# Loading the first 512 tokens of an attention and feed-forward kernel in longer rows

## The chip, the cores and the metric

The kernel runs on one core of a Trainium2 chip. The metric is device time in microseconds (us) of one launch. A core has five engines that run side by side and wait for each other through semaphores: PE (TensorE, matrix products and transposes; its weight loads are a row of their own, PEld), DVE (VectorE), ACT (ScalarE), POOL (GpSimd) and SP (SyncE, which here only issues transfers). Transfers between HBM and the on-chip memory run on 16 DMA engines.

## What is computed

Attention inside chunks of 64 tokens, for 8 batches of 8 heads, 576 tokens and 64 features, and then a feed-forward layer with a squared ReLU over all 4608 tokens:

```python
B, H, S, D = q.shape            # 8, 8, 576, 64; float32
q_c = q.reshape(B, H, S // 64, 64, D)          # k, v likewise
scores = (1 / sqrt(D)) * matmul(q_c, k_c.transpose(0, 1, 2, 4, 3))
attn = softmax(scores, axis=-1)
a = matmul(attn, v_c).reshape(B, H, S, D)
x = a.transpose(0, 2, 1, 3).reshape(B * S, H * D)   # 4608 x 512
out = maximum(x @ w_in, 0) ** 2 @ w_out             # d_ff 2048; float32 out
```

## The kernel before

The tokens are numbered through all batches and cut into 18 groups of 256 (`GT`). Two groups make a block of 512 tokens; there are nine: groups 0 and 1, then 3 and 2, then 4 and 5, and so on. For each block the kernel does the attention of its groups, and then the two products of the feed-forward layer: `ffn_in` (L316 on PE, ReLU on ACT at L322, square on DVE at L323, 16 steps) and `ffn_out` (L332), for block 0 `ffn_out_by_ft` (L361). The output leaves through ACT copies and POOL's DMAs.

The attention of a group has these steps. q and k come in as float32 in `q_sb` and `k_sb`, the values in `v_even` (even heads) and `v_odd` (odd heads, shifted by 64 tokens so that the chunks of both kinds lie on different halves of the partitions); each row of values carries an element 1.0 behind its 64 features, so that the product gives the sum of the softmax as well. q and k are turned so that the features lie on partitions (`qkT`). For groups 0 to 3 PE does this on the upper halves of the float32 words, read as bfloat16 (L164), and DVE and ACT copy it out of PSUM (L173). For later groups POOL casts (L212) and a transposing DMA does the rest (L219). `scores` makes 32 products of 64x64 (L233) and one exponential on ACT (L240). `values` makes, for each of the two tiles of 128 tokens, 16 products of 64x65 (L257), a reciprocal (L264) and a product (L265) on DVE, which gives `x`. `x` is transposed into `xT`, by PE for groups 0 to 5 (L195 and L284), by a transposing DMA from group 6 on (L278).

The order of everything is written out by hand: each engine works through its instructions in program order. At the beginning the loads of groups 0 and 1 are issued on SP's queue (q, k of group 0, of group 1, then the values of both), then the first piece of `w_in`, and then PE goes through the attention of groups 0 and 1. Between the steps stand fillers, `keep_busy(n)`: n products of the identity with itself, 128 columns each, whose result nobody reads. Then come the rest of `w_in` (8 pieces in all, cast to bfloat16 by POOL at L139) and `w_out` (8 pieces, L147) through five staging buffers (`w_st`), and the loads of group 3 and 2. After that the blocks follow, with the attention of the next block and the loads of the one after it spliced into slots of the feed-forward steps.

For groups 0 to 3 two neighbouring tokens of a head lie on one partition (512 B in HBM, one row of a transfer); the copy out of PSUM puts the tokens back in order. For later groups a row of q or k is one token of a head, 256 B, as are the rows of the values in all groups. The number of rows of a transfer is partitions x heads. All loads are issued by SP, in program order.

The text below names these: `qk_pieces` (L102, L110) and `v_pieces` (L117, L124) issue the loads, `load_w_in` (L136, L139) and `load_w_out` (L144, L147) the weights, `transpose_qk` is called as TE for groups 0 and 1, TA for group 3 and TM for group 2.

Of the kernel before, what the change touches and what calls it, by code (L numbers as in the profile page):

```python
# [10 lines left out]
FP32 = mybir.dt.float32  # L11
BF16 = mybir.dt.bfloat16
AF = mybir.ActivationFunctionType
ALU = mybir.AluOpType
# [3 lines left out]
def kernel(  # L18
# [9 lines left out]
    nc = tc.nc  # L28

    B, H, S, D = q.shape  # L30
    n_tokens = B * S
# [3 lines left out]
    n_hp = H // 2  # L35
    n_dt = d_model // 128
    n_ft = d_ff // 128
    GT = 256
    n_grp = n_tokens // GT

    blocks = [[0, 1], [3, 2]] + [[g, g + 1] for g in range(4, n_grp, 2)]
    FIRST_DMA_T = 4
    FIRST_DMA_X = 6
    BT = GT * max(len(b) for b in blocks)

    const_pool = ctx.enter_context(tc.tile_pool(name="const", bufs=1))
# [7 lines left out]

    ctx.enter_context(tc.manual_schedule())

    ident_f32 = const_pool.tile([128, 128], FP32, name="ident_f32")
    make_identity(nc, ident_f32)
    ident = const_pool.tile([128, 128], BF16, name="ident")
# [7 lines left out]
    NO = 2 * NV + 1  # L67
    v_even = [w_pool.tile([128, 2, n_hp, D + 1], FP32, name=f"ve_sb{i}") for i in range(NV)]
    v_odd = [w_pool.tile([128, n_hp, D + 1], FP32, name=f"vo_sb{i}") for i in range(NO)]
    for vt in v_even:  # L70
        nc.gpsimd.memset(vt[:, :, :, D:D + 1], 1.0)
    for vt in v_odd:
# [2 lines left out]
    def segments(g0, n):  # L75
        while n:
            b, s = divmod(g0, S)
            m = min(n, S - s)
            yield b, s, m
            g0 += m  # L80
            n -= m
# [9 lines left out]
                p += m  # L91

    def qk_pieces(g):
        q_sb = in_pool.tile([128, 2, H, D], FP32, name="q_sb")
        k_sb = in_pool.tile([128, 2, H, D], FP32, name="k_sb")
        qk[g] = (q_sb, k_sb)
        if g < FIRST_DMA_T:

            p = 0
            for b, s, m in segments(g * GT, GT):  # L100
                for dst, src in ((q_sb, q), (k_sb, k)):
                    yield lambda dst=dst, src=src, b=b, s=s, p=p, m=m: nc.sync.dma_start(  # L102
                        out=dst.rearrange("p t h d -> p (t h d)")[p:p + m // 2, :].rearrange(
                            "p (h e) -> p h e", h=H),
                        in_=src[b, :, s:s + m, :].rearrange("h (s i) d -> s h (i d)", i=2))
                p += m // 2
            return
        for t, p, m, b, s in runs(g):
            for dst, src in ((q_sb, q), (k_sb, k)):
                yield lambda dst=dst, src=src, b=b, s=s, t=t, p=p, m=m: nc.sync.dma_start(  # L110
                    out=dst[p:p + m, t, :, :],
                    in_=src[b, :, s:s + m, :].rearrange("h s d -> s h d"))

    def v_pieces(g):

        for t, p, m, b, s in runs(g):
            yield lambda t=t, p=p, m=m, b=b, s=s: nc.sync.dma_start(  # L117
                out=v_even[g % NV][p:p + m, t, :, 0:D],
                in_=v[b, 0::2, s:s + m, :].rearrange("h s d -> s h d"))
        for n in {0: [0, 1, 2], 2: [5], 3: [6, 7, 8]}.get(g, [2 * g + 1, 2 * g + 2]):  # L120
            lo, hi = max(0, 128 * n - 64), min(n_tokens, 128 * n + 64)
            p = lo - (128 * n - 64)
            for b, s, m in segments(lo, hi - lo):
                yield lambda n=n, p=p, m=m, b=b, s=s: nc.sync.dma_start(  # L124
                    out=v_odd[n % NO][p:p + m, :, 0:D],
                    in_=v[b, 1::2, s:s + m, :].rearrange("h s d -> s h d"))
                p += m
# [47 lines left out]
    def transpose_qk(g, q_pool, k_pool):  # L175
        qkT = att_pool.tile([128, 2, 2, n_hp, 128], BF16, name="qkT", bufs=4)
        state["qkT", g] = qkT
        for which, pool in enumerate((q_pool, k_pool)):
            copy = nc.scalar.copy if which else nc.vector.tensor_copy
            if pool is ps_ffn:  # L180
                bank = pool.tile([128, 512], FP32, name="ps_ffn")
            else:
                bank = pool.tile([128, 1024], FP32, name="ps_att")
            bank = bank.bitcast(BF16)[:, 0:1024]
            transpose_paired(g, which, bank)
            copy_paired(copy, qkT[:, which], bank)

    def transpose_x_early(g, t):
        j, c = place[g]
        if j not in xTs:  # L190
            xTs[j] = att_pool.tile([128, BT // 128, n_dt, 128], BF16, name="xT", bufs=2)
        psb = ps_ffn.tile([128, 512], FP32, name="ps_ffn").bitcast(BF16)
        x = state["x", g]
        for hp in range(n_hp):
            nc.tensor.transpose(  # L195
                out=psb[:, hp * 128:(hp + 1) * 128],
                in_=x[:, t, hp].rearrange("p a d -> p (a d)"),
                identity=ident)
        copy = nc.vector.tensor_copy if t else nc.scalar.copy
        copy(  # L200
            out=xTs[j][:, c // 128 + t].rearrange("p h q -> p (h q)"), in_=psb[:, 0:512])

    def keep_busy(n):
        ps = ps_ffn.tile([128, 512], FP32, name="ps_ffn")
        for _ in range(n):
            nc.tensor.matmul(out=ps[:, 0:128], lhsT=ident, rhs=ident, start=True, stop=True)

    def cast_qk(g):
        qkb = att_pool.tile([128, 2, 2 * H * D], BF16, name="qkb", bufs=2)
# [13 lines left out]
    def scores(g):  # L223
        qkT = state.pop(("qkT", g))
        ps = ps_att.tile([128, 1024], FP32, name="ps_att")
        for hp in range(n_hp):
            for t in range(2):
                for a in range(2):
                    for p in range(2):
                        c = p ^ a  # L230
                        cols = slice(p * 64, p * 64 + 64)
                        o0 = a * 512 + hp * 128 + t * 64
                        nc.tensor.matmul(  # L233
                            out=ps[64 * c:64 * c + 64, o0:o0 + 64],
                            lhsT=qkT[64 * a:64 * a + 64, 1, t, hp, cols],
                            rhs=qkT[64 * a:64 * a + 64, 0, t, hp, cols],
                            start=True, stop=True)
        e = att_pool.tile([128, 2, n_hp, 2, 64], BF16, name="e")
        state["e", g] = e
        nc.scalar.activation(  # L240
            out=e.rearrange("p a h t q -> p (a h t q)"), in_=ps, func=AF.Exp, scale=scale)

    def values(g, tiles=(0, 1)):
        e = state["e", g]
        veb = v_even[g % NV].bitcast(BF16)
        vob = [v_odd[(2 * g + n) % NO].bitcast(BF16) for n in range(3)]
        if 0 in tiles:
            state["x", g] = att_pool.tile([128, 2, n_hp, 2, D], BF16, name="x", bufs=3)
        x = state["x", g]
        for t in tiles:  # L250
            ps = ps_att.tile([128, 2, 512], FP32, name="ps_att")
            for hp in range(n_hp):
                for a in range(2):
                    for p in range(2):
                        c = p ^ a
                        vb = vob[t + p] if a else veb[:, t]
                        nc.tensor.matmul(  # L257
                            out=ps[64 * p:64 * p + 64, a, hp * (D + 1):(hp + 1) * (D + 1)],
                            lhsT=e[64 * c:64 * c + 64, a, hp, t, :],
                            rhs=vb[64 * c:64 * c + 64, hp, 1::2],  # L260
                            start=True, stop=True)
            o = ps[:, :, 0:n_hp * (D + 1)].rearrange("p a (h d) -> p a h d", d=D + 1)
            rec = att_pool.tile([128, 2, n_hp], FP32, name="rec", bufs=4)
            nc.vector.reciprocal(out=rec, in_=o[:, :, :, D])  # L264
            nc.vector.tensor_tensor(  # L265
                out=x[:, t].rearrange("p h a d -> p a h d"),
                in0=o[:, :, :, 0:D],
                in1=rec.to_broadcast([128, 2, n_hp, D]),
                op=ALU.mult)
# [24 lines left out]
    def TA(g):  # L294
        transpose_qk(g, ps_att, ps_att)

    def TE(g):
        transpose_qk(g, ps_ffn, ps_ffn)

    def TM(g):  # L300
        transpose_qk(g, ps_att, ps_ffn)

    def XE(g):
        for t in range(2):
            transpose_x_early(g, t)

    gTs = {}

# [76 lines left out]

    go(pieces([0, 1]))
    load_w_in(0, n_cast=2)
    TE(0)
    keep_busy(8)
    SC(0)  # L390
    keep_busy(6)
    TE(1)
    keep_busy(8)
    SC(1)
    keep_busy(10)
    AV(0, [0])
    keep_busy(4)
    AV(0, [1])
    keep_busy(8)
    transpose_x_early(0, 0)  # L400
    keep_busy(10)
    transpose_x_early(0, 1)
    AV(1, [0])
    keep_busy(8)
    AV(1, [1])
    transpose_x_early(1, 0)
    keep_busy(14)
    transpose_x_early(1, 1)
    keep_busy(10)

    for i in range(1, 8):
        load_w_in(i)
# [90 lines left out]
```

The softmax here doesn't subtract the row's maximum and nothing guards it: scores larger than these inputs give would overflow.

## Time and profile before

| | |
|---|---|
| median of 8 runs | 297.78 us |
| lowest and highest | 295.26 and 303.7 us |
| profiled execution, device time | 303.7 us |
| its span, first to last instruction | 301.9 us |
| its mean granted PE clock | 0.986 |
| PE, DVE, ACT, POOL busy | 284.8, 113.9, 131.0, 67.7 us |
| HBM read, written | 36.70, 9.44 MB |
| first L164 on PE | 4.99 us |
| first cast of `w_in` on POOL | 18.25 us |
| first L316 of block 0 | 20.13 us |

The profile is of one execution, the slowest of the eight; times in it count from its first instruction. The busy share of an engine says how much of the span it worked, not whether it was waited for; that is told by the waits and by the chain that ended last. In the rows by slice the span is cut into 40 equal parts of 7.5 us and a digit is a busy share in tenths. In the view by windows each engine has its busy time in the stretch and, in brackets, its instructions; then come the granted PE clock, the mean busy share of the DMA engines and the rate in GB/s.

### The profile page before, as it was taken

The page shows a single profiled execution, that of the slowest core. Times are in us where ns is not written, and L with a number is a line of the kernel's source. Part 1 is how long each engine was busy: PE and PEld are TensorE (multiplying, and loading weights), DVE is VectorE, ACT ScalarE, POOL GpSimd, SP SyncE. Part 2 cuts the span into 40 slices and gives each one's busy share as a digit, 9 for nine tenths or more (in the row PEclk, how much of TensorE's full clock was granted, in tenths as well). Part 3 has the DMA queues.
Part 4 walks back from the last instruction along what each step waited for, and adds up shares of the span by engine and source line. Part 5 has one row for each costly group of instructions (what it writes and reads, how often), then busy time and mean ns, then how long its engine had stood idle before and what let it go on. Part 6 is the DMA issues. An engine that isn't in the chain of part 4 may idle for free.

```text
span 301.9 us, 6460 instructions
## 1 busy us (share of the span) xinstructions
PE 284.8 (94%) x2630; PEld 142.4 (47%) x2630; DVE 113.9 (38%) x246; ACT 131.0 (43%) x226; POOL 67.7 (22%) x103
## 2 busy tenths in 40 slices
PE   2899998999899995999999999999999999999994
PEld 2674454885444442344444444444444444444441
DVE  1258514682434520247026604540563045205300
ACT  1536414773337511373157315721671267126511
POOL 2047724140070061032206013201320100010010
PEclk9999999999999999699999999999999999999998
DMA  7999999999999999999999699779996600310011
GB/s 208 217 322 363 362 292 244 241 215 204 207 213 208 226 228 209 230 201 182 208 262 223 124 257 253 151 149 267 226 164 134 181 35 14 92 72 35 0 69 69
DMA packets 156141, 57.03 MB, mean 189 GB/s; under 512 B 139281, under 2 KB 151825, under 8 KB 156113
## 3 DMA queue, kind: packets, MB, share of 16 engines
q1 hardware_dynamic: 153168, 47.33, 75.1%
q0 software_dynamic: 2800, 9.18, 9.1%
q8 instruction: 20, 0.33, 0.5%
q10 hardware_dynamic: 144, 0.13, 0.1%
q14 instruction: 9, 0.07, 0.1%
HBM read 36.70 MB, written 9.44 MB: 153 GB/s over the span
## 4 chain that ended last, share of the span: by engine, by line
PE 75%; DMA 12%; SPq 8%; DVE 1%; issue 1%; POOL 1%; ACT 0%; ACTq 0%
PE ps_ffn L316 37%; PE ps_ffn L332 34%; DMA w_st<-in_moe_w_in_dram 4%; DMA k_sb<-in_k_dram 2%; SPq L124 2%; DMA w_st<-in_moe_w_out_dram 2%; SPq L102 2%; DMA xT<-x 2%; PE ps_att L257 2%; SPq L117 2%; PE ps_att L233 2%; DMA qkT<-qkb 1%; SPq L136 1%; POOL w_in_bf L139 1%; DVE gT L323 1%
## 5 line engine op out<-in xcount | busy, mean ns | idle before, releaser
L316 PE MATMUL ps_ffn<-xT,w_in_bf 128*128 128x512 bf16 (+1 forms) x640 | 131.8, 363 | 4.0 <-DMA xT<-x 3.3
L323 DVE TENSOR_TENSOR gT<-rl 128x512 bf16<-128x512 bf16 (+1 forms) x160 | 76.5, 492 | 132.9 <-ACT rl L322 130.7
L332 PE MATMUL ps_ffn<-w_out_bf,gT 128*128 128x512 bf16 x512 | 112.9, 379 | 0.0
L322 ACT ACTIVATE rl<-ps_ffn 128x512 bf16<-128x512 f32 (+1 forms) x160 | 86.6, 557 | 44.2 <-PE ps_ffn L316 38.7
L316 PEld LDWEIGHTS <-w_in_bf 128*128 128x128 bf16 x640 | 61.8, 99 | 65.9 <-issue 4.8
L332 PEld LDWEIGHTS <-gT 128*128 128x128 bf16 x512 | 49.3, 98 | 58.0
L349 ACT COPY o_sb<-ps_ffn 128x512 f32<-128x512 f32 x31 | 18.2, 586 | 91.5 <-PE ps_ffn L332 91.5
L350 POOL DMA_DIRECT2D out_dram<-o_sb x31 | 16.7, 539 | 141.8 <-ACT o_sb L349 141.8
L212 POOL CAST qkb<-q_sb 128x1024 bf16<-128x1024 f32 x14 | 14.8, 1057 | 52.9 <-DMA q_sb<-in_q_dram 48.2
L265 DVE TENSOR_TENSOR x<-ps_att,rec 128x512 bf16<-128x512 f32 x36 | 24.9, 692 | 1.2
L240 ACT ACTIVATE e<-ps_att 128x1024 bf16<-128x1024 f32 x18 | 17.9, 1023 | 5.3 <-PE ps_att L233 5.2
L212 POOL CAST qkb<-k_sb 128x1024 bf16<-128x1024 f32 x14 | 15.5, 1110 | 2.5 <-DMA k_sb<-in_k_dram 2.3
L361 PE MATMUL ps_ffn<-w_out_bf,gT 128*128 128x512 bf16 x64 | 14.7, 379 | 0.0
L264 DVE RECIPROCAL rec<-ps_att 128x8 f32<-128x8 f32 x36 | 7.2, 200 | 16.6 <-PE ps_att L257 16.6
L139 POOL CAST w_in_bf<-w_st 128x1024 bf16<-128x1024 f32 (+1 forms) x9 | 8.6, 959 | 19.4 <-DMA w_st<-in_moe_w_in_dram 19.4
L257 PEld LDWEIGHTS <-e 64*64 64x64 bf16 x576 | 6.6, 107 | 8.3 <-issue 2.3
L147 POOL CAST w_out_bf<-w_st 128x1024 bf16<-128x1024 f32 x8 | 8.9, 1112 | 7.2 <-DMA w_st<-in_moe_w_out_dram 7.1
L257 PE MATMUL ps_att<-vo_sb,e 64*64 64x65 bf16 x288 | 9.1, 196 | 1.0 <-DMA vo_sb<-in_v_dram 1.0
L361 PEld LDWEIGHTS <-gT 128*128 128x128 bf16 x64 | 6.0, 98 | 7.2 <-DVE gT L323 0.3
L257 PE MATMUL ps_att<-ve_sb,e 64*64 64x65 bf16 x288 | 9.1, 197 | 0.0
L233 PE MATMUL ps_att<-qkT 64*64 64x64 bf16 x576 | 7.7, 197 | 1.4 <-DMA qkT<-qkb 1.0
L233 PEld LDWEIGHTS <-qkT 64*64 64x64 bf16 x576 | 6.0, 110 | 6.2 <-issue 3.2
(34 smaller groups left out, 53.4 us busy)
## 6 DMA issues: line engine op xcount, KB each, us to landing
out_dram<-o_sb POOLq DMA_DIRECT2D x35, 256.0 KB, 4.1
q_sb<-in_q_dram SPq DMA_DIRECT2D x25, 256.0 KB, 5.0
k_sb<-in_k_dram SPq DMA_DIRECT2D x25, 256.0 KB, 5.0
ve_sb<-in_v_dram SPq DMA_DIRECT2D x32, 128.0 KB, 4.1
vo_sb<-in_v_dram SPq DMA_DIRECT2D x32, 128.0 KB, 3.7
w_st<-in_moe_w_in_dram SPq DMA_DIRECT2D x8, 512.0 KB, 6.5
w_st<-in_moe_w_out_dram SPq DMA_DIRECT2D x8, 512.0 KB, 6.6
q_sb<-in_q_dram SPq DMA_DIRECT2D x3, 512.0 KB, 6.7
```

The lines of the kernel that those rows point to most:

```text
L212: nc.gpsimd.tensor_copy(out=qkb[:, which], in_=qk[g][which].rearrange("p t h d -> p (t h d)"))
L233: nc.tensor.matmul(out=ps[64 * c:64 * c + 64, o0:o0 + 64], lhsT=qkT[64 * a:64 * a + 64, 1, t, hp, cols], rhs=qkT[64 * a:64 * a + 64, 0, t, ...
L240: nc.scalar.activation(out=e.rearrange("p a h t q -> p (a h t q)"), in_=ps, func=AF.Exp, scale=scale)
L257: nc.tensor.matmul(out=ps[64 * p:64 * p + 64, a, hp * (D + 1):(hp + 1) * (D + 1)], lhsT=e[64 * c:64 * c + 64, a, hp, t, :], rhs=vb[64 * c: ...
L265: nc.vector.tensor_tensor(out=x[:, t].rearrange("p h a d -> p a h d"), in0=o[:, :, :, 0:D], in1=rec.to_broadcast([128, 2, n_hp, D]), op=AL ...
L316: nc.tensor.matmul(out=h[:, 0:n], lhsT=w_in_bf[:, dt, ft * 128:(ft + 1) * 128], rhs=xT[:, c // 128:(c + n) // 128, dt, :], start=(dt == 0) ...
L322: nc.scalar.activation(out=rl[:, 0:n], in_=h[:, 0:n], func=AF.Relu)
L323: nc.vector.tensor_tensor(out=gT[:, ft, c:c + n], in0=rl[:, 0:n], in1=rl[:, 0:n], op=ALU.mult)
L332: nc.tensor.matmul(out=o_ps, lhsT=gT[:, ft, tt * 128:(tt + 1) * 128], rhs=w_out_bf[:, ft, :], start=(ft == 0), stop=(ft == n_ft - 1))
L349: nc.scalar.copy(out=o_sb, in_=o_ps)
L350: nc.gpsimd.dma_start(out=out[t0:t0 + 128, :], in_=o_sb)
L361: nc.tensor.matmul(out=o_ps[tt], lhsT=gT[:, ft, tt * 128:(tt + 1) * 128], rhs=w_out_bf[:, ft, :], start=(ft == 0), stop=(ft == n_ft - 1))
```

## The change

Only the first 512 tokens (groups 0 and 1) are treated differently.

- q of both groups comes in one transfer of 128 partitions, four neighbouring tokens of a head on one partition (1 KB rows), and so does k. `qk[0]` is q of 512 tokens, `qk[1]` is k. Both lie in `qk_sb`, which for the other groups holds q and k of one group as two halves.
- The values of a group come in one transfer, two neighbouring tokens of a head on one partition (512 B rows), all heads together, in `v_pair`. A row has an element 1.0 at its front and at its end.
- `transpose_both` does what TE did, for q of both groups and then for k of both: 32 transposes into two PSUM banks, copied by DVE (bank 0) and ACT (bank 1), once per group.
- Since a partition of `v_pair` holds an even and an odd token, the keys of a chunk of 64 are split into 32 even and 32 odd ones. `scores` makes 64 products of 64x32 (32 keys) for 64 queries each instead of 32. `values` makes for a tile 32 products over 32 keys, which accumulate, and four products of zeros ahead of them that clear the accumulators; the two columns of ones give two partial sums, which a reduction on DVE adds ahead of the reciprocal.
- `keep_busy` multiplies zeros, 512 columns wide, and its counts are others: 12 of them stand ahead of the first transpose.
- The part of `v_odd` that group 1 loaded for group 2 (64 tokens) is loaded with group 2's values.
- SP issues 4 transfers ahead of the first piece of `w_in` instead of 13.

```diff
@@ tiles
+    zeros = const_pool.tile([128, 512], BF16, name="zeros")
+    nc.gpsimd.memset(zeros, 0.0)
+    v_pair = [w_pool.tile([128, H, 2 * D + 2], FP32, name=f"vp_sb{i}")
+              for i in range(N_PAIRED)]
+    for vt in v_pair:
+        nc.gpsimd.memset(vt[:, :, 0:1], 1.0)
+        nc.gpsimd.memset(vt[:, :, 2 * D + 1:2 * D + 2], 1.0)
@@ qk_pieces
-        q_sb = in_pool.tile([128, 2, H, D], FP32, name="q_sb")
-        k_sb = in_pool.tile([128, 2, H, D], FP32, name="k_sb")
+        qk_sb = in_pool.tile([128, 2, 2, H, D], FP32, name="qk_sb")
+        if g < 2:
+            qk[g] = qk_sb.rearrange("p w t h d -> p (w t h d)").rearrange(
+                "p (h e) -> p h e", h=H)
+            p = 0
+            for b, s, m in segments(0, 2 * GT):
+                yield lambda dst=qk[g], src=(q, k)[g], b=b, s=s, p=p, m=m: nc.sync.dma_start(
+                    out=dst[p:p + m // 4],
+                    in_=src[b, :, s:s + m, :].rearrange("h (s i) d -> s h (i d)", i=4))
+                p += m // 4
+            return
+        q_sb, k_sb = qk_sb[:, 0], qk_sb[:, 1]
@@ v_pieces
+        if g < N_PAIRED:
+            p = 0
+            for b, s, m in segments(g * GT, GT):
+                yield lambda b=b, s=s, p=p, m=m: nc.sync.dma_start(
+                    out=v_pair[g][p:p + m // 2, :, 1:2 * D + 1],
+                    in_=v[b, :, s:s + m, :].rearrange("h (s i) d -> s h (i d)", i=2))
+                p += m // 2
+            return
-        for n in {0: [0, 1, 2], 2: [5], 3: [6, 7, 8]}.get(g, [2 * g + 1, 2 * g + 2]):
-            lo, hi = max(0, 128 * n - 64), min(n_tokens, 128 * n + 64)
+        for n in {2: [4, 5], 3: [6, 7, 8]}.get(g, [2 * g + 1, 2 * g + 2]):
+            lo, hi = max(N_PAIRED * GT, 128 * n - 64), min(n_tokens, 128 * n + 64)
@@ new: q (which = 0) or k (which = 1) of groups 0 and 1
+    def transpose_both(which):
+        nh = n_hp // 2
+        src = qk[which].bitcast(BF16).rearrange("p h (i d) -> p h i d", i=4)
+        copies = []
+        for part, copy in enumerate((nc.vector.tensor_copy, nc.scalar.copy)):
+            bank = ps_ffn.tile([128, 512], FP32, name="ps_ffn").bitcast(BF16)
+            dst = bank.rearrange("c (h i q) -> c h i q", h=nh, i=4)
+            for hp in range(nh):
+                for i in range(4):
+                    for a in range(2):
+                        nc.tensor.transpose(
+                            out=dst[64 * a:64 * a + 64, hp, i, :],
+                            in_=src[:, 2 * (part * nh + hp) + a, i, 1::2],
+                            identity=ident)
+            of = bank.rearrange("c (h i g t p) -> c g t h p i", h=nh, i=4, g=2, t=2)
+            copies.append((copy, slice(part * nh, part * nh + nh), of))
+        for g in range(2):
+            if which == 0:
+                state["qkT", g] = att_pool.tile(
+                    [128, 2, 2, n_hp, 128], BF16, name="qkT", bufs=4)
+            for copy, hs, of in copies:
+                to = state["qkT", g][:, which, :, hs].rearrange(
+                    "c t h (p i) -> c t h p i", i=4)
+                copy(out=to, in_=of[:, g])
@@ keep_busy
-            nc.tensor.matmul(out=ps[:, 0:128], lhsT=ident, rhs=ident, start=True, stop=True)
+            nc.tensor.matmul(out=ps, lhsT=zeros[:, 0:128], rhs=zeros, start=True, stop=True)
@@ scores, for g < N_PAIRED
+            for hp in range(n_hp):
+                for i in range(2):
+                    for c in range(4):
+                        t, p = divmod(c, 2)
+                        for a in range(2):
+                            o0 = a * 512 + hp * 128 + i * 64
+                            nc.tensor.matmul(
+                                out=ps[32 * c:32 * c + 32, o0:o0 + 64],
+                                lhsT=qkT[64 * a:64 * a + 64, 1, t, hp,
+                                         p * 64 + i:p * 64 + 64:2],
+                                rhs=qkT[64 * a:64 * a + 64, 0, t, hp, p * 64:p * 64 + 64],
+                                start=True, stop=True)
@@ values, for g < N_PAIRED, each tile t
+                for a in range(2):
+                    for p in range(2):
+                        rows = slice(64 * t + 32 * p, 64 * t + 32 * p + 32)
+                        nc.tensor.matmul(
+                            out=ps[64 * p:64 * p + 64, a, 0:n_hp * E],
+                            lhsT=zeros[rows, 0:64], rhs=zeros[rows, 0:n_hp * E],
+                            start=True, stop=False)
+                for hp in range(n_hp):
+                    for a in range(2):
+                        for i in range(2):
+                            for p in range(2):
+                                rows = slice(64 * t + 32 * p, 64 * t + 32 * p + 32)
+                                nc.tensor.matmul(
+                                    out=ps[64 * p:64 * p + 64, a,
+                                           hp * E + i:hp * E + i + D + 1],
+                                    lhsT=e[rows, a, hp, i, :],
+                                    rhs=vp[rows, 2 * hp + a,
+                                           2 * i * (D + 1) + 1:2 * (i + 1) * (D + 1):2],
+                                    start=False, stop=(i == 1 and hp == n_hp - 1))
+                nc.vector.tensor_reduce(
+                    out=rec, in_=o[:, :, :, 0:D + 2:D + 1], axis=mybir.AxisListType.X,
+                    op=ALU.add)
+                nc.vector.reciprocal(out=rec, in_=rec)
...
@@ the order at the beginning
-    TE(0)
-    keep_busy(8)
+    keep_busy(12)
+    transpose_both(0)
+    keep_busy(4)
+    transpose_both(1)
+    keep_busy(2)
     SC(0)
-    keep_busy(6)
-    TE(1)
-    keep_busy(8)
+    keep_busy(1)
     SC(1)
-    keep_busy(10)
+    keep_busy(4)
     AV(0, [0])
-    keep_busy(4)
     AV(0, [1])
-    keep_busy(8)
+    keep_busy(3)
     transpose_x_early(0, 0)
-    keep_busy(10)
+    keep_busy(2)
     transpose_x_early(0, 1)
     AV(1, [0])
-    keep_busy(8)
     AV(1, [1])
     transpose_x_early(1, 0)
-    keep_busy(14)
+    keep_busy(3)
     transpose_x_early(1, 1)
-    keep_busy(10)
+    keep_busy(2)
```

## The prediction

> **What bounds the kernel now.** I read the page's busy rows first, then the waits of PE, then the chain that ended last, then the window view in stretches of 1 us, and last the timeline of the first 21 us. PE is busy for 94% of the span, so what can be gained is what PE waits for. The waits of PE name it:
>
> ```profile
> PE ps_ffn L164 <- DMA q_sb<-in_q_dram: 5.0, 1, 5.0
> PE ps_ffn L316 <- DMA xT<-x: 3.3, 1, 3.3
> PE ps_att L233 <- DMA qkT<-qkb: 1.0, 1, 1.0
> ```
>
> The columns are total us, times, longest. With the waits on k and v (1.5 and 1.0 us in two each, of which 0.78 at 52.0 us and 0.47 at 48.3 us by the timeline) every wait of weight is for a transfer. The page's slices say why:
>
> ```profile
> DMA  7999999999999999999999699779996600310011
> GB/s 208 217 322 363 362 292 244 241 215 204 207 213 208 226 228 209 230 201 182 208 262 223 124 257 253 151 149 267 226 164 134 181 35 14 92 72 35 0 69 69
> ```
>
> The DMA engines are full up to about 166 us, and SP's queue issues without a real gap until 125 us: the first 120 us are one transfer chain beside one PE chain, and PE waits where the former is late. The rate depends on the row of the stretch:
>
> ```profile
> 7.00:8.00 1.00, 1.00 (x19) 0.83 (x16) 0.39 (x1) 0.12 (x1) 0.00 (x0) 1.00 1.20 290
> 11.00:12.00 1.00, 0.90 (x22) 0.64 (x16) 1.00 (x2) 0.61 (x2) 0.00 (x0) 1.00 1.40 178
> 14.00:15.00 1.00, 0.45 (x19) 0.23 (x17) 0.83 (x2) 0.02 (x1) 0.00 (x0) 1.00 0.76 123
> 24.00:25.00 1.00, 1.00 (x6) 0.49 (x5) 0.84 (x2) 0.73 (x2) 0.57 (x2) 1.00 1.11 350
> 120.00:121.00 1.00, 0.60 (x2) 0.28 (x3) 0.00 (x0) 0.00 (x0) 0.00 (x0) 0.50 1.31 147
> ```
>
> The last column is GB/s, the third from the end PE's clock. q and k in 512 B rows run at 290; v in 256 B rows at 178 to 227, mean 208 over 10 to 14 us; w_in in 1 KB rows at 350. Between v and w_in (14 to 16 us) there is a hole: 123 and 216 GB/s, 1.0 us lost against 350. The last row shows what the longest wait costs beyond itself: after 3.3 us without work PE restarts at 120.4 us with the clock at 0.50, until about 126.1 us, so 5.7 us run at half speed and 2.9 us are lost. The chain shows the same place:
>
> ```profile
> 114.27 6.08 DMA xT<-x
> 120.40 11.67 PE ps_ffn L316 x40
> ```
>
> From there to the end PE waits for no transfer.
>
> [...]
>
> **The change, part by part: transfers.** q and k are 2.10 MB: 7.2 us at 290, 6.0 at 350, saves 1.2. v of groups 0, 1 was 1.11 MB with 64 odd-head tokens of group 2: 5.4 us at 208; now 1.05 MB at 290, 3.6, saves 1.7. The 64-token piece (66 KB, 0.3 us) returns as one more DMA with group 2's values. SP issues 4 DMAs instead of 13 ahead of w_in, so w_in is queued behind v early and the 1.0 us hole should close; I take it as closed, bounds 0 and 1.0. Cross-check from the front: the first q landed at 4.99 us, issued at 0.73, 1.8 us of data, so 2.45 us are fixed. Then q lands at 0.73 + 2.45 + 3.0 = 6.2 us, k at 9.2, v at 11.0 and 12.8, the first w_in at 14.3, cast at 18.25 before: 3.9 earlier, 3.6 once the 64-token piece is paid. The lead passes down the queue: from the sixth weight piece on a transfer waits for a cast on POOL (1.0 us), which follows its own landing, and block 0 uses a piece in 1.73 us (8 matmuls of 0.216) while one lands each 1.5. So the chain of transfers leads by **3.6 us**, between 2.7 and 3.9.
>
> **PE's prologue.** Before, PE starts on q at 4.99 and on block 0's L316 at 20.13. After:
>
> PE first runs 12 matmuls of 512 columns on zeros; at half clock they are 0.43 us apart (the spacing at 121 us), 5.1 us from about 1.2 us, which POOL's memset of zeros sets (128x128 took 0.2 us; 0.2 to 0.8 for this one). They end at 6.3, when q lands[...]. The ident, later by that memset, is used only then.
>
> All 32 transposes of q and their copies fit before k lands at 9.2. k's 32 take twice 0.64 us less the overlap, 1.1, to 10.3. The copies are as many elements as before: DVE 0.65 us each, ACT 0.54; the first group's end at 10.85, the second's at 11.4.
>
> Scores of group 0: 64 matmuls instead of 32. The nearest row is 0.45 us for 32; I take 0.7, between 0.45 and 1.9. Exp (1.02 us) runs 11.6 to 12.6, that of group 1 to 13.65. PE does group 1's scores and 4 filler matmuls (0.86 us) until 13.2, so the first values start there, against 13.53 before: v has landed.
>
> Values: per tile 4 zeroing matmuls of 264 columns and 32 of 65, for 16 before: 0.6 us, between 0.4 and 1.8. DVE then has a reduce, a reciprocal and a product per tile: the reduce has no row; with its 16 inputs it is near the reciprocal's 0.20 us (bounds 0.1 and 0.4). One tile is 0.2 + 0.2 + 0.69 + gaps = 1.15 us instead of 0.93. Tiles end at 15.0 and 16.15; transposes and the xT copy go to 17.0; group 1's values stand behind that transpose on PE, so its tiles end at 18.3 and 19.4; transposes 0.4, copy 0.42, gaps: L316 starts at **20.4**, 0.3 later than before. Bounds: 19.0 with cheap small matmuls and a short reduce, 22.5 with dear ones. What is queued behind these waits on PE is the whole of block 0, so every us here moves all of PE.
>
> The fillers of 512 columns (21 after the first 12, 0.216 us each, 4.5 us, for 86 of 128 columns at 0.054, 4.6 us) mostly fill waits; I charge the 0.86. The added memsets on POOL (0.1 us each) end long before the first cast. From 20 us on no instruction of PE, DVE or ACT is added. q and k of one group now share one buffer, which is returned only when both are read; the loads concerned come tens of us after that.
>
> **The sum.** PE is 0.3 later, transfers 3.6 earlier. The waits at 48.3, 52.0 and 75.3 us (0.47, 0.78, 1.04) are each shorter than the new lead and go: 2.3 us. What is late next is PE itself. At 117 us PE arrives 2.0 earlier, xT up to 3.6 earlier: the 3.3 us wait shrinks to 1.7, too short to reach the clock's fall 2.2 us into it, so the 2.9 us go too. In the profiled execution (303.7 us, span 301.9 and 1.8 around it) that is 303.7 + 0.3 - 2.3 - 1.7 - 2.9 = 297.1. But that execution lies 5.9 above the median of 297.78, and its wait at 117 us with the slow clock is 6.2: I read the median as an execution nearly without these, 297.5, in which the small waits stand. So 297.5 + 0.3 - 2.3 = 295.5; with the 0.3 between 297.5 and the median half counted, **295.6 us**.
>
> **Rivals.** (a) The lead serves no wait: in the median execution the small waits are absent, as the fastest run, 295.26, is hardly above the 295.2 that the profile leaves without any of them. Then only the prologue shows: 297.8 + 0.3 = 298.1. For it speaks that a wait of 0.5 us is within what two executions may differ by; against it, that the median is 2.5 above that floor and something must fill it. (b) Slower: the prologue's PE chain. 208 small matmuls lie on the path (scores of group 0 and four value tiles); I price them at 11 to 17 ns each. At about 17 ns more each, L316 starts at 24, 3.9 late, and the end is 297.7 - 2.3 + 3.9 = 299.3; that is the point. A weight load alone has a mean of 107 ns, so if loads of 32-row tiles are not hidden it is passed by far; I put this case at 300.5. For it: [...] DVE's longer tile; against it, that 64x64 loads are hidden today. (c) The rows don't do what they say: 1 KB as slow as 512 B. Then k lands 1.2 later, L316 at 21.6, the lead is 2.4: 295.6 + 1.2 = 296.8.
>
> **Numbers.** A difference of 0.5%, 1.5 us, is about what a measurement of this kernel can tell from no change: faster is below 296.3, slower above 299.3. Forecast 0.58 (own range 294.0 to 296.6), (c) 0.10, (a) 0.18, (b) 0.14. Faster takes 0.55 of the forecast and 0.05 of (c) for its spread: 0.60; same 0.03 + 0.05 + 0.17 = 0.25; slower 0.14 and 0.01 of (a): 0.15. The range is 293.8 to 299.2: below it the case that all waits vanish and the prologue is at its short bound, above it most of (b).
>
> **What would show it.** Right: the first cast of w_in near 14.5 us and no hole ahead of it; L316 starting within 19 to 22 us; no wait of PE for k at 52 us or qkT at 75 us; a wait for xT near 115 us under 2.2 us and no 0.50 clock. Wrong: L316 at 24 us or later; a w_in cast after 16 us; the waits of 48 to 76 us still there with the transfers earlier.

## The result, and the profile after

The changed kernel is slower: 301.85 us median (301.13 to 303.86, 11 runs) against 298.63 us for the kernel before (32 runs), a ratio of 1.0154 with a 95% interval of 1.0121 to 1.0186. The forecast was 295.6 us with a range of 293.8 to 299.2, so the result lies outside it and on the other side. The 8 runs that the forecast started from had a median of 297.78; over 32 runs it is 0.85 higher. Ratios here and below compare only those runs of each kernel that lie within 1.5% of its fastest, so they are not the quotients of the medians. The profiled execution took 301.85 us, its span is 299.8 us.

New line numbers: the feed-forward product L316 is now L412 (ReLU L322 is L418, square L323 is L419), the values of groups 0 and 1 are L336 with their zeroing matmuls at L327, those of later groups L360, POOL's cast of q and k is L265, its output DMA L473, the fillers L259.

The waits of PE in the kernel after (total us, times, longest):

```profile
PE ps_att L336 <- issue: 3.3, 1, 3.3
PE ps_att L360 <- ACT e L307: 1.9, 1, 1.9
PE ps_ffn L259 <- POOL zeros L59: 1.3, 1, 1.3
PE ps_ffn L226 <- DMA qk_sb<-in_k_dram: 0.7, 1, 0.7
```

Every late DMA that the prediction named is gone: there is no wait for k at 52 us, for qkT, or for xT. Two other waits stand at the head of the list. "issue" means that the profile shows nothing that PE waited for.

The slices of the kernel after, 7.5 us each:

```profile
PEclk9959999999999999999999999999999999999998
DMA  7999999999589969999999899699976701210011
GB/s 244 349 381 396 347 230 224 292 173 215 149 172 237 223 139 234 235 229 168 217 265 218 118 216 268 151 134 232 271 174 135 182 37 27 80 70 37 0 70 70
```

Slices 2 to 5 move 347 to 396 GB/s, where before they moved 217 to 363: the transfers lead as forecast. But PE's clock is halved in the third slice. The window view there (PE, PEld, DVE, ACT, POOL, then PE's clock, DMA share, GB/s) says when:

```profile
13.00:14.00 1.00, 0.43 (x9) 0.34 (x9) 0.00 (x0) 0.16 (x1) 0.26 (x1) 1.00 1.10 389
14.00:15.00 1.00, 0.00 (x0) 0.00 (x0) 0.00 (x0) 0.00 (x0) 0.91 (x2) 1.00 1.10 382
15.00:16.00 1.00, 0.00 (x0) 0.00 (x0) 0.00 (x0) 0.00 (x0) 0.00 (x0) 0.50 1.08 371
...
20.00:21.00 1.00, 1.00 (x7) 0.71 (x6) 0.00 (x1) 0.32 (x1) 0.72 (x2) 0.50 1.06 366
21.00:22.00 1.00, 1.00 (x10) 0.53 (x10) 0.04 (x1) 0.27 (x1) 0.68 (x2) 0.58 1.09 383
22.00:23.00 1.00, 1.00 (x55) 0.99 (x52) 0.55 (x2) 0.00 (x0) 0.90 (x1) 1.00 1.09 402
```

No engine but POOL works from 14 to 15 us and none from 15 to 16, while the DMA engines are full. PE's timeline (start, length, line, instructions, idle time before):

```profile
12.95 0.41 PE L327 MATMUL ps_att<-zeros 32*64 32x264 bf16 x4
13.20 0.23 PE L336 MATMUL ps_att<-vp_sb,e 32*64 32x65 bf16 x4
16.71 0.81 PE L336 MATMUL ps_att<-vp_sb,e 32*64 32x65 bf16 x23 [3.28 <-issue]
...
26.09 1.24 PE L412 MATMUL ps_ffn<-xT,w_in_bf 128*128 128x512 bf16 x5 [0.18 <-DVE xT L253]
```

PE starts the values at 12.95 us, does four of a tile's 32 products, and stands still for 3.28 us in the middle of a row of equal instructions, with no operand that the profile shows to be late. Block 0 starts at 26.09 us; before it was 20.13, forecast was 20.4.

The second wait is at 61 to 63 us. The timeline of four engines there:

```profile
57.09 0.54 POOL L473 DMA_DIRECT2D out_dram<-o_sb  x1 [0.32 <-DMA vo_sb<-in_v_dram]
57.62 3.98 POOL L265 CAST qkb<-qk_sb 128x1024 bf16<-128x1024 f32 x4
59.07 3.49 DVE L419 TENSOR_TENSOR gT<-rl 128x256 bf16<-128x256 bf16 x4 [0.53 <-ACT rl L418]
61.85 0.38 ACT L418 ACTIVATE rl<-ps_ffn 128x256 bf16<-128x256 f32 x1 [2.26 <-DVE gT L419]
62.13 1.02 ACT L307 ACTIVATE e<-ps_att 128x1024 bf16<-128x1024 f32 x1
63.20 0.22 PE L360 MATMUL ps_att<-ve_sb,e 64*64 64x65 bf16 x2 [1.92 <-ACT e L307]
```

POOL runs four casts back to back, and while they run one of DVE's squares takes 2.69 us (by the instructions of tile gT) where its neighbours take 0.29. ACT's ReLU needs the buffer which that square frees, the exponential stands behind the ReLU on ACT, and PE's values of group 2 wait for it.

### The profile page after: what moved, and what is told of

Same layout as the page of the kernel before. It is cut to its first block, busy times and chain, and to the rows that moved or that the text cites. A ratio compares the mean times of both kernels' runs of the same rounds, so it can differ in the third digit from the quotient of the medians.

```text
span 299.8 us, 6638 instructions
## 1 busy us (share of the span) xinstructions
PE 287.6 (96%) x2721; PEld 142.0 (47%) x2721; DVE 114.6 (38%) x250; ACT 131.2 (44%) x226; POOL 67.7 (23%) x108
## 4 chain that ended last, share of the span: by engine, by line
PE 93%; DMA 3%; DVE 2%; issue 1%; ACT 1%; SPq 0%; ACTq 0%
PE ps_ffn L412 41%; PE ps_ffn L428 37%; PE ps_ffn L457 5%; DMA qk_sb<-in_k_dram 3%; PE ps_att L360 2%; PE ps_att L300 2%; PE ps_ffn L259 2%; DVE gT L419 1%; PE ps_att L336 1%; PE ps_att L387 1%; PE ps_ffn L248 1%; PE ps_att L191 1%; PE ps_att L287 0%; PE ps_ffn L226 0%; ACT e L307 0%
## 5 line engine op out<-in xcount | busy, mean ns | idle before, releaser
L412 PE MATMUL ps_ffn<-xT,w_in_bf 128*128 128x512 bf16 (+1 forms) x640 | 128.9, 358 | 0.2 <-DVE xT L253 0.2
L419 DVE TENSOR_TENSOR gT<-rl 128x512 bf16<-128x512 bf16 (+1 forms) x160 | 76.5, 494 | 126.9 <-ACT rl L418 123.6
L418 ACT ACTIVATE rl<-ps_ffn 128x512 bf16<-128x512 f32 (+1 forms) x160 | 87.1, 558 | 38.8 <-PE ps_ffn L412 33.4
L412 PEld LDWEIGHTS <-w_in_bf 128*128 128x128 bf16 x640 | 61.2, 98 | 60.0 <-POOL w_in_bf L166 0.6
L265 POOL CAST qkb<-qk_sb 128x1024 bf16<-128x1024 f32 x28 | 29.5, 1081 | 28.3 <-DMA qk_sb<-in_q_dram 22.8
L368 DVE TENSOR_TENSOR x<-ps_att,rec 128x512 bf16<-128x512 f32 x32 | 22.1, 692 | 1.1
L259 PE MATMUL ps_ffn<-zeros 128*128 128x512 bf16 x33 | 11.4, 480 | 1.3 <-POOL zeros L59 1.3
L367 DVE RECIPROCAL rec<-ps_att 128x8 f32<-128x8 f32 x32 | 6.4, 199 | 13.2 <-PE ps_att L360 13.2
L360 PEld LDWEIGHTS <-e 64*64 64x64 bf16 x512 | 5.5, 107 | 8.6 <-ACT e L307 2.6
L360 PE MATMUL ps_att<-ve_sb,e 64*64 64x65 bf16 x256 | 7.3, 195 | 1.9 <-ACT e L307 1.9
L360 PE MATMUL ps_att<-vo_sb,e 64*64 64x65 bf16 x256 | 7.3, 195 | 0.0
L300 PEld LDWEIGHTS <-qkT 64*64 64x64 bf16 x512 | 4.9, 108 | 4.0 <-issue 3.6
L336 PE MATMUL ps_att<-vp_sb,e 32*64 32x65 bf16 x128 | 3.7, 213 | 3.3 <-issue 3.3
```

The costliest lines, as they stand in the source:

```text
L259: nc.tensor.matmul(out=ps, lhsT=zeros[:, 0:128], rhs=zeros, start=True, stop=True)
L265: nc.gpsimd.tensor_copy(out=qkb[:, which], in_=qk[g][which].rearrange("p t h d -> p (t h d)"))
L360: nc.tensor.matmul(out=ps[64 * p:64 * p + 64, a, hp * (D + 1):(hp + 1) * (D + 1)], lhsT=e[64 * c:64 * c + 64, a, hp, t, :], rhs=vb[64 * c: ...
L368: nc.vector.tensor_tensor(out=x[:, t].rearrange("p h a d -> p a h d"), in0=o[:, :, :, 0:D], in1=rec.to_broadcast([128, 2, n_hp, D]), op=AL ...
L412: nc.tensor.matmul(out=h[:, 0:n], lhsT=w_in_bf[:, dt, ft * 128:(ft + 1) * 128], rhs=xT[:, c // 128:(c + n) // 128, dt, :], start=(dt == 0) ...
L418: nc.scalar.activation(out=rl[:, 0:n], in_=h[:, 0:n], func=AF.Relu)
```

## Two theories for the stop at 13 us

**Theory 1, PE's instructions were not there.** The page lists DMA queues by kind (packets, MB, share of the 16 engines). Two are of the kind "instruction"; in the first 55 us one of them brings only 56 B, so the other counts here. This is its line in the kernel before and in the kernel after:

```profile
q8 instruction: 20, 0.33, 0.5%
q8 instruction: 21, 0.34, 0.5%
```

Each packet has 16,384 B. I counted PE's records in the trace (weight loads and products, and the two or three drain and semaphore records ahead of block 0, in order of their start; below they are called listed instructions) and put the packets beside them. In the kernel before, one packet starts at 12.38 us, after PE's 195th instruction (10.74), and the next at 18.20, after its 449th (16.69). In the kernel after, the 195th is at 10.49, PE stops after the 449th at 13.24, the packet is there from 14.37 to 15.33, and PE goes on at 16.71. So I took it that PE does not get past its 449th listed instruction before the first packet has come, and stands still if it is there earlier. That is my estimate from these counts and times; what a packet holds and what makes it start the profile does not show. The 195th is a mark from which I count the packet's delay: 254 listed instructions ahead of the 449th, after which the next packet starts in the kernel before. The counts do not carry on: in three traces (the kernel before, and two below, even keys and count alone) the third packet starts 0.1, 3.3 and 0.9 us ahead of the 703rd. The change adds some 180 listed instructions ahead of block 0 (from about 588 to 770) and packs them densely (195th to 449th in 2.75 us instead of 5.95). In the same stretch, from 12 to 14 us, the DMA engines move 379 and 389 GB/s instead of 227 and 222, and the packet starts 3.88 us after the 195th instead of 1.64.

**Theory 2, the values do it themselves:** the 32-row tiles, their accumulation in PSUM or a hidden dependence stall PE at that instruction.

For the 1.9 us at 61 us the theory (theory 3 below) was that the row of casts on POOL holds up DVE's square: the one of 2.69 us runs while the four casts take 3.98 us, and 2.69 us is more than two of them. By what means they would do so the trace does not show.

## The experiments

Each edit is to the kernel after, unless it says otherwise. Ratios are against the kernel before, run beside it.

**Small fillers first.** If the stop belongs to a count, other instructions ahead of it move it to another place in the work.

```diff
-    keep_busy(12)              # 12 products of 512 columns
+    keep_busy_small(96)        # 96 products of 64 columns, zeros
```

> The changed kernel with its first 12 fillers (512 columns) replaced by 96 of 64 columns: the same PE time, 168 PE instructions (a weight load and a product for each filler) more, all of them before q lands. Theory 1, instruction supply: PE stood from 13.24 to 16.71 us because its next instructions were not there; a 16 KB packet of the instruction queue came at 14.37 us[...]. With 168 instructions more ahead of q [...] the packet comes before 12 us, the values of group 0 have no gap, L316 of block 0 starts at 20 to 21.5 us instead of 26.1, and the time falls by 4 to 6 us, to 296 to 298. Theory 2, the gap belongs to the values (first products of 32 rows, v or its ones late): it stays at the fifth product of the values, L316 starts near 26 us, time 301 to 304.

Measured: 302.55 us (20 runs), ratio 1.0079 (1.003 to 1.0129). The expectation of no stop was wrong. The waits of PE:

```profile
PE ps_att L342 <- issue: 2.9, 1, 2.9
...
PE ps_att L293 <- issue: 1.0, 2, 0.8
```

The first packet did come early (9.42 us), but now PE stops twice: inside the scores of group 1 (L293) after its 448th instruction, 11.17 to 12.13, and inside the second tile of values (L342) after its 702nd, 15.26 to 18.33, with a second packet at 15.91, 3.78 us after the 449th at 12.13. So the stop moved away from the place where it was and into other operations, and stayed at the counts. That speaks against theory 2. I had overlooked that a stop at the 449th can be followed by another some 254 listed instructions on, with the second packet.

**w_in held back** until group 0's exponential, so that none of its rows are on their way when the packet comes.

```diff
+            nc.gpsimd.tensor_copy(out=st[:, 0, 0:2], in_=after[:, 0, 0, 0, 0:2])
...
-    load_w_in(0, n_cast=2)     # stood ahead of the first filler
     SC(0)
+    load_w_in(0, n_cast=2, after=state["e", 0])
```

> The changed kernel with the loads of w_in held until the exponential of group 0 is done (near 12.2 us): the DMA engines are idle from about 12 us on for some 2 us. Theory 1: the packet of instructions waits behind w_in's rows of 1 KB; without them it comes at 12 to 12.5 us, PE's gap shrinks from 3.5 us to 0 to 1.5 us, L316 starts at 20.5 to 22.5 us, 297 to 299 us. Theory 2: gap and start as in the changed kernel (26 us), 301 to 304. A third, that the packet comes late whatever the transfers do: the gap stays at 3 us or more.

Measured: 299.28 us, ratio 1.0044 (1.0016 to 1.0073). The packet came at 11.88 us, 1.19 after the 195th instead of 3.88, and the first stop shrank to 1.07 us. But then w_in's 1 KB rows came (its first cast was at 15.93 us), the second packet took 4.64 us from the 449th, and PE stopped for 2.69 us after its 701st, which I had not foreseen:

```profile
21.53 0.52 PE L338 MATMUL ps_att<-vp_sb,e 32*64 32x65 bf16 x21 [2.50 <-issue]
```

Block 0 started at 24.66, later than expected.

**q and k alone** in 1 KB rows; the values of groups 0 and 1 as before.

```diff
-    N_PAIRED = 2
+    N_PAIRED = 0
```

> The q and k part alone: q, k jointly in 1 KB rows with transpose_both, the fillers of the changed kernel; values in 256 B rows and products of 64 keys as before. PE has some 310 instructions up to the first values instead of 440, and the rows of v, not of w_in, fill the DMA engines until 13.5 us. Theory 1: no gap or one under 1 us; L316 starts at 20 to 21.5 us (v of group 1 lands near 14 us), w_in near 16 us; 295.5 to 298.5. Theory 2: no gap either, since the values are the old ones. So this run tells what part 1 is worth.

Measured: 296.76 us (20 runs), ratio 0.988 (0.9847 to 0.9913): faster than both kernels. The longest of PE's waits:

```profile
PE ps_att L300 <- DMA qkT<-qkb: 2.8, 2, 2.0
```

No stop on "issue" at all before block 0; the clock stays at 1.00 from 6.1 us on; block 0 starts at 18.91 us, 1.2 earlier than before and 1.1 earlier than I expected. Both theories forecast no stop here, so the run tells what the part is worth, not which theory holds. Some late transfers remain; v keeps its slow rows here.

**The values alone** as in the kernel after; q, k, their transposes and the fillers as before.

> The values' part alone: v of groups 0, 1 in 512 B rows, tiles of 32 keys; q, k, their transposes, the order and the fillers as before. Theory 1: PE reaches some 450 instructions at the first values near 13 us[...]; the packet comes while v's 512 B rows run, a shorter wait than behind 1 KB rows: a gap of 0 to 2 us. Theory 2: the gap stays at 3 us at the fifth product of the values. L316 starts at 21 to 23 us (theory 1) or 24 and more (theory 2); 297 to 300 or above 300.

Measured: 301.55 us, ratio 1.0135 (1.01 to 1.017). PE stops at its 449th instruction for 1.28 us, this time in a filler, a product of the identity that has nothing to do with values:

```profile
14.64 0.22 PE L259 MATMUL ps_ffn<-ident 128*128 128x128 bf16 x1 [1.06 <-issue]
```

The clock is at 0.50 from 17.1 to 20.6 us, block 0 starts at 24.86, and the 1.9 us at 60 to 62 us are there as in the kernel after. The start and the time fall where I had put theory 2; the length of the stop and its place speak for theory 1. The loss comes with the values' part and does not need the longer rows of q and k. With the small fillers of before this kernel has some 876 listed instructions ahead of block 0.

**Even keys only.** This leaves out the odd keys of groups 0 and 1, with the same loads, the same rows and the same 32-row tiles but half the products.

```diff
-                for i in range(2):       # scores
+                for i in range(1):       # and 128 columns of queries for 64
...
-                        for i in range(2):   # values
+                        for i in range(1):
```

> The changed kernel with the odd keys of groups 0 and 1 left out: per group 32 score products of 64x32 with 128 columns instead of 64 with 64 columns, per tile 16 value products instead of 32; loads, tile shapes, fillers and order as in the changed kernel. That is 256 PE instructions fewer before block 0. Theory 1 [...]: PE comes to its 449th instruction near 16.5 us instead of 13.2, after the packet; no gap above 1 us, L316 of block 0 at 19.5 to 21.5 us, 295 to 298.5 us. Rival: the cost is that of 32-row and 32-column tiles or of the longer q and k rows; then L316 starts at 24 us or later, 300 us or more.

Measured: 295.52 us (20 runs), ratio 0.9895 (0.987 to 0.9921). PE's timeline and the windows:

```profile
20.17 0.59 PE L412 MATMUL ps_ffn<-xT,w_in_bf 128*128 128x512 bf16 x2 [0.18 <-POOL w_in_bf L166]
```

```profile
13.00:14.00 1.00, 1.00 (x40) 0.84 (x37) 0.55 (x3) 0.12 (x1) 0.14 (x1) 1.00 1.08 383
14.00:15.00 1.00, 0.97 (x7) 0.43 (x7) 0.93 (x4) 0.00 (x0) 1.00 (x2) 1.00 1.12 389
```

The packet is as late as in the kernel after (3.82 us, at 14.48), the DMA engines are as full, but PE reaches the 449th only at 16.70, after the packet's end at 15.46: no stop, and no half clock there. The run can't tell by itself whether it is the count or the work of the odd keys that matters; the last run does.

**Casts held back.** Group 4's casts wait for group 2's exponential, by a copy on POOL of two elements per partition.

```diff
+        if g == 4:
+            nc.gpsimd.tensor_copy(out=qkb[:, 0, 0:2], in_=state["e", 2][:, 0, 0, 0, 0:2])
```

> The changed kernel with POOL's casts of q, k of groups 4 and 5 held until the exponential of group 2 is done, by one copy of two columns ahead of them. Theory 3: four casts in a row from 57.6 us stop DVE (one square of 256 columns took 2.69 us instead of 0.29), so ACT, the exponential and PE's values of group 2 wait 1.9 us. Then without casts at 57 to 61 us that wait falls below 0.5 us; the casts slow later squares, at 62 to 67 us, where PE has slack of two tiles: the time falls by 0.5 to 2 us against the changed kernel (301.85). Rival: the wait comes from something else (ACT behind the PSUM copies); then it stays at 1.5 us or more and the time too. The gap at the 449th instruction stays.

Measured: 301.1 us (4 runs), ratio 1.0133 (1.0095 to 1.0172).

```profile
PE ps_att L338 <- issue: 3.2, 1, 3.2
PE ps_att L389 <- DVE x L370: 1.0, 2, 0.6
```

Four squares at 59.20 take 1.16 us together instead of 3.49, and the 1.9 us wait is gone, so the casts are its cause; by what means they slow the square no run here tells. But the casts then run from 61.39 to 65.6 and slow three later squares to 2.38 us, so that PE waits 1.0 us for `x`. The median is 0.75 us below that of the kernel after, which is within the spread of its runs, and the intervals of the two ratios overlap. In the profiled executions the stretch from block 0 to the end is 0.5 us shorter: of a wait of 1.9 us that was moved, little comes back.

**w_in in 256 B rows** for the first two pieces: the same bytes in rows a quarter as long.

```diff
-        nc.sync.dma_start(out=st, in_=moe_w_in[:, cols]...)
+        if i < 2:
+            for c in range(0, 256, 64):
+                nc.sync.dma_start(out=st[:, :, c:c + 64], ...)
+        else:
+            nc.sync.dma_start(out=st, in_=moe_w_in[:, cols]...)
```

> The changed kernel with the first two pieces of w_in in rows of 256 B (four transfers each) instead of 1 KB. The DMA engines are as full as before at 12 to 17 us. If the packet of instructions waits behind the rows that stand in the same engine's queue, it waits for fewer bytes: it comes 1 to 2 us earlier than 14.4 us, PE's gap at the 449th instruction shrinks to 1 to 2.5 us. If only the fullness counts, packet and gap stay (14.4 us, 3.5 us). w_in lands some 2 us later either way, not later than 17 us, L316 at 24 to 26.5; time 300 to 302.5.

Measured: 298.81 us (7 runs), ratio 1.0003 (0.9945 to 1.0061). The packet starts at 12.79 us, 2.06 after the 195th, the stop is 1.59 us, and block 0 starts at 23.74; start and time are a little better than expected.

```profile
15.06 0.55 PE L344 MATMUL ps_att<-vp_sb,e 32*64 32x65 bf16 x23 [1.39 <-issue]
```

The DMA engines' busy share from 11 to 13 us is 1.21 and 1.32, against 1.15 and 1.08 in the kernel after. So the engines were not less busy there when the packet came earlier.

**The count by itself.** To the kernel with q and k alone, which has no stop, 64 tiny products of zeros are added in place of four fillers; values, transfers and DVE's work are those of that kernel.

```diff
     SC(1)
-    keep_busy(4)               # 4 products of 512 columns
+    keep_busy_small(64)        # 64 products of 64x64 by 64 columns, zeros
     AV(0, [0])
```

> The kernel with q and k alone in 1 KB rows, in which 4 fillers of 512 columns ahead of the first values (0.86 us of PE) are replaced by 64 products of zeros, 64x64 by 64 columns, at the 14 ns of a product of the scores about 0.9 us: equal time of PE, 120 more listed instructions (weight loads and products), nothing else changed; values, transfers and DVE work stay. Theory 1 (PE stops where its instructions have not come): the 449th listed instruction comes inside the values of group 0 or the filler behind them, near 14 us instead of 15.8 us; the packet of instructions still comes near 12.6 to 13.9 us[...]; PE resumes near 15.2 us: a stop of 0.8 to 1.6 us at a count of 446 to 449 that nothing else explains, and block 0 starts 0.5 to 2 us later than the 18.91 us of the kernel without the edit. Rival (the values over 32 keys themselves, or their longer DVE steps, make PE wait): no such stop here, since the values are those of before, and block 0 starts near 18.9 us.

Measured: there is one run, 297.47 us, so only its trace is used. The timeline of PE shows

```profile
12.15 2.12 PE L264 MATMUL ps_ffn<-zeros 64*64 64x64 bf16 x62
...
14.21 0.23 PE L366 MATMUL ps_att<-ve_sb,e 64*64 64x65 bf16 x2
15.60 0.22 PE L366 MATMUL ps_att<-ve_sb,e 64*64 64x65 bf16 x2 [1.17 <-issue]
```

The old 64-row values, which stop nowhere in the kernel without the edit, now stop after PE's 448th instruction and stand idle for 1.17 us. The packet ran from 12.78 to 14.02. The stop is as theory 1 expected; block 0 starts at 21.37 instead of 18.91, 2.46 later and a little more than expected, as the tiny products took 2.1 us where I had put 0.9. The first values start 1.05 us later for that (14.09 instead of 13.04), and the stop of 1.36 us, from start to start, makes up nearly all of the rest.

Put together from the traces (us; a stop is counted from the start of one instruction to the start of the next; "195th" is the start of that listed instruction, the mark for the packet's delay):

| kernel | 195th | packet | PE at its 446th to 449th | stop | block 0 starts |
|---|---|---|---|---|---|
| before | 10.74 | 12.38–13.68 | 16.69 | none | 20.13 |
| after | 10.49 | 14.37–15.33 | 13.24 | 3.47 | 26.09 |
| small fillers | 6.26 | 9.42–10.51 | 11.17 | 0.96, later 3.07 | 26.65 |
| w_in held | 10.70 | 11.88–13.04 | 13.4 | 1.07, later 2.69 | 24.66 |
| q, k alone | 11.04 | 12.63–13.87 | 15.84 | none | 18.91 |
| values alone | 8.89 | 11.90–13.03 | 13.36 | 1.28 | 24.86 |
| even keys | 10.67 | 14.48–15.46 | 16.70 | none | 20.17 |
| casts held | 10.60 | 14.30–15.19 | 13.35 | 3.34 | 26.21 |
| w_in in 256 B | 10.73 | 12.79–13.72 | 13.5 | 1.59 | 23.74 |
| count alone | 11.21 | 12.78–14.02 | 14.24 | 1.36 | 21.37 |

Where PE reaches that count more than 1.2 us after the packet's end (before, q and k alone, even keys) it doesn't stop; where it comes earlier (before the packet's end, or up to 0.7 us after it) it stops, and goes on 1.3 to 1.6 us after the packet's end. Theory 2 has no account of stops in scores, in a filler and in the old values. What stays open is what sets the packet's delay. The kernels whose 195th comes at 10.5 to 10.7 us can be compared without knowing what makes the packet start: the first packet came at 11.88 with w_in held back, at 12.38 and 12.79 among 256 B rows, and at 14.30 to 14.48 among 1 KB rows. Counted from the 195th, or for the second packet from the 449th or PE's restart there, it took 1.2 us with w_in held back, 1.6 to 2.1 among 256 B rows and 2.9 to 4.6 among longer ones. An exception is the second packet of the kernel before, 1.5 us after the 449th among w_in's 1 KB rows; the engines' share fell to 0.79 there. Why the packet comes later among longer rows was not shown.

## Why the prediction was wrong

**Transfers: right.** The first cast of w_in was at 13.74 us (forecast 14.3 to 14.5), k's transposes started at 8.88 (k forecast at 9.2), the hole ahead of w_in closed. All the late transfers went, xT's wait fully where 1.7 us of it were to stay. From the start of block 0 to the end of the span the kernel before took 281.8 us, 9.1 of them in waits (6.2) and lost at half clock (2.9); the kernel after took 273.7.

**Prices of PE and DVE: right.** 64 scores took 0.68 us (0.7), a tile's reduce, reciprocal and product 1.14 us (1.15), the first values started at 12.95 (13.2). With even keys alone, block 0 started at 20.17, within 0.3 us of the forecast's 20.4, and the time was 295.52. That kernel makes half of the small products, so it agrees with the forecast's chain where PE does not stop, but doesn't test it in full.

**The step that failed** is the one from there to "L316 starts at 20.4": the tiles of values that "end at 15.0 and 16.15" and what follows them. It left no room for a stop of PE amid instructions whose operands are there. Measured, L412 starts at 26.09, 5.7 later. About 3.5 us of it is the stop. The other 2.2 us is put down to the clock, which fell 1.8 us into the idle time and stayed at 0.50 until 21.8 us, 5.1 us after the restart, so that some 2.5 us of PE's work was lost; in the kernel of the count alone, whose clock stayed at 1.00, no such loss came on top of the stop. The bound of 22.5 us covered dear matmuls, not such a stop. The count was in reach, as the code has some 180 more of PE's instructions ahead of block 0, and so was the page's third part with its queue of the kind "instruction" (20 packets, 0.33 MB); that the count bears on the time only the runs showed.

**A second term was missing**, 1.9 us, in "What is late next is PE itself". POOL's casts of groups 4 and 5 stand behind its four output DMAs, which wait for block 0. These lines are POOL's timeline, first of the kernel before, then with even keys alone:

```profile
51.82 0.54 POOL L377 DMA_DIRECT2D out_dram<-o_sb  x1 [0.32 <-ACT o_sb L375]
59.62 1.07 POOL L212 CAST qkb<-q_sb 128x1024 bf16<-128x1024 f32 x1 [7.26 <-DMA q_sb<-in_q_dram]
```

```profile
51.70 1.05 POOL L265 CAST qkb<-qk_sb 128x1024 bf16<-128x1024 f32 x1
53.17 1.18 POOL L265 CAST qkb<-qk_sb 128x1024 bf16<-128x1024 f32 x1 [0.41 <-DMA qk_sb<-in_k_dram]
58.06 2.36 POOL L265 CAST qkb<-qk_sb 128x1024 bf16<-128x1024 f32 x2 [3.71 <-DMA qk_sb<-in_q_dram]
```

Before, the casts wait for their data. With the lead alone they come one or two at a time as the data lands, and PE doesn't wait. In the kernel after the data is early and PE 6 us late, so when the output DMAs end at 57.62 all four are ready, and they run in a row beside DVE's squares. The wait thus comes of the first stop together with the lead. The lead without the stop did not give it. Nor did a late PE with later data: with w_in held or in 256 B rows, block 0 starts at 24.66 and 23.74, the casts run two by two, 4.23 and 3.65 us apart, waiting for q, and the wait on the exponential isn't there.

**The sum**, on the profiled executions: forecast 297.1, measured 301.85, a difference of 4.75. The late start gives +5.7, the casts +1.9. From block 0 to the end the forecast left 297.1 − 1.8 − 20.4 = 274.9 us; measured, without the 1.9, it was 271.8, so −3.1: 1.7 of it is the part of xT's wait that the forecast left standing, 0.6 a wait on ACT's ReLU at 62 us that it did not take off, and 0.8 was not traced. That gives 4.5, and 0.25 lies outside the span (2.05 us instead of 1.8). The 295.6 that the forecast gave for the median is 1.5 lower mainly because it had no wait for xT left in it.

**The rivals.** (b) named the right place and the right mark, L316 at 24 us or later, but not the mechanism: the small matmuls cost what the forecast gave them, and it is their number that costs. (a) is refuted: with even keys alone block 0 starts where it did before, and yet the ratio is 0.9895, so the lead did serve waits. (c) is refuted: k's transposes started at 8.88 us, not 1.2 later than forecast. The listed sign "L316 at 24 us or later" is the one that came.

## What to carry to other kernels

Count an engine's instructions as well as their time. Here 64 tiny products in place of four fillers were enough for a stop of 1.36 us in values that had none, and in the kernel after, which came to its 449th listed instruction 1.13 us before the packet started, PE stood for 3.47 us. In the profile that looks like a wait on "issue" amid equal instructions, with the instruction queue's packet inside it or just ahead of it. Keep the part of a change that pays without such a stop: here the 1 KB rows of q and k with their transposes and fillers, at 0.988 of the time before. And when one chain is made to lead, look at what starts together once the lead meets an engine that still keeps its old order, such as casts piled up behind an output.

## What the runs showed of the hardware that I had not expected

- PE's stops lie after 446 to 449 and 701 or 702 listed instructions, 254 or 255 apart, in the kernels above. By weight loads alone, which are more fully on record than products, they lie after 223 or 224 and after 352, and where PE stops twice it goes on the second time only after the second packet of 16,384 B: with the small fillers that packet starts at 15.91 us, and PE goes on at 18.33. Ahead of block 0 a packet takes 0.9 to 1.3 us, and PE goes on 1.3 to 1.6 us after its end.
- The packet came later with w_in's 1 KB rows on their way: 1.19 us after PE's 195th listed instruction with w_in held back, 3.7 to 3.9 us with it in those rows, and 4.64 us from the 449th to the second packet once the held w_in came.
- Four casts in a row on POOL kept one square of DVE for 2.69 us instead of 0.29.
- The 32-row and 32-column tiles are cheap: 64 products of 64x32 took 0.68 us against 0.45 for 32 of 64x64, and a tile's 32 products over 32 keys took 0.69 us. The small fillers of zeros were dearer than their size: 62 products of 64x64 by 64 columns, all into one place of PSUM, took 2.12 us, 34 ns each instead of 14; why was not tried.
